# Eight vector additions handed to accumulating GpSimd transfers, with a new instruction order: attention fused with a gated FFT convolution on one Trainium2 core

## The chip, the cores and the metric

The kernel runs on one core of one Trainium2 chip. The time is the device time of one execution in microseconds (us). The engines are TensorE (PE), VectorE (DVE), ScalarE (ACT), GpSimd (POOL) and SyncE (SP); each works through its own instructions in the order in which they were emitted, and waits on semaphores for the others. DMAs are issued by SP and ACT (hardware queues) and by GpSimd (a software queue), and run on the core's 16 DMA engines.

## The reference, cut to what matters

```python
# attention: batch 4, 8 heads, 768 positions, 64 per head
scores = scale * q @ k^T + bias(head, distance)      # bias falls with the distance
keep   = (pos < 8) | (0 <= row - pos < 96)           # 8 global keys and a window of 96
a      = softmax(where(keep, scores, -1e9))
x      = (a @ v), heads joined                       # [4, 768, 512]
# gated convolution over the sequence
x1, x2, x3 = split(x @ w_proj, 3)                    # 512 columns each
X2 = rfft(x2, n=768, axis=1);  H = rfft(filter_fft, n=768, axis=0)
y  = x1 * irfft(X2 * H, n=768, axis=1) * x3
return (y @ w_out).astype(float32)                   # [4, 768, 512]
```

The part that the change touches is `X2 * H`, a product of complex numbers, and the last folding steps of `irfft`.

## The kernel before

The work of each of the four batches (index `b` from 0 to 3 in the code; the text of the change calls index 1 batch 2 and index 2 batch 3) is an attention part and a convolution part. The program puts the attention of batch `b + 1` among the convolution of batch `b`.

**Attention.** The 768 positions are cut into key tiles of 112, in three groups (`GRP`). GpSimd loads q, k and v from HBM, casting float32 to float16 (`load`, L325). PE turns q and k tiles (`turned`, L679; the very first tiles come in float32 and are turned at L647), then computes scores for a pair of heads (`scores`: the biases of the first batch at L707, the scores at L720), with 64 rows per matmul, two heads side by side. ACT takes the exponentials (L748), DVE multiplies by a mask (L760), PE multiplies by v (`values`, L778 and L783), DVE takes reciprocals and scales (`xn`, L802, L808), PE turns the result (`trx`, L825) or SP does by a transposing DMA (`crossed_x`). `gate` (L870) projects x1 and x3; the gates `g` are their product (L881).

**Convolution.** DVE folds the turned x (`butterfly`, L846 to L857). The projection of x2 (L944) is evacuated to `ab`. `spectra` makes spectra on PE (`forward`, L634) with short Fourier matrices: six slots `X[:, 0..5]` of 512 columns. Slots (0, 1) and (2, 3) are real and imaginary parts of a complex product with the filter: DVE multiplies X by the filter's real part `h1` into `p1`, by `h2` (imaginary part, once with a minus sign) into `p2`, and adds `p1` and `p2` with its two halves swapped into X (`sums`, L1098). Slots 4 and 5 are done apart (L1081, L1084). PE then goes back (`inv`, L965 and L968; three slots and `p3` per matrix) into `eo`. `mixed` unfolds `eo` on DVE: `u` and `w` (sums and differences of the odd parts, L1036 and L1037), `t = z - u` (`mt`, L1038), `u` doubled (`mu`), `z = z + u` (`mz`, L1040), `s = t - w` (`m1`, L1041), `t = t + w` (`m2`, L1042). `gated` joins even and odd parts (`half`, L1056 and L1057) and multiplies with the gates (L1061). `out` projects with `w_out` (L996), the result is evacuated to `ot` and stored by SP (L1003). The in-place `z` and `t` are parts of `eo` of 128 columns at a step of 384; X, `p1` and `p2` are contiguous over two slots, 1024 float16 numbers per partition.

**The order.** Every step is an operation (`Op`) of a plan, numbered in the order in which `graph` creates it, with the engines that may do it, a cost for the planner, what it reads and writes. `ORDER` is a string that was written by a search outside the program. Each of its words is an operation number, the engine that does it (P, A, V, G, S) and, for matmuls, the PSUM banks. `schedule` reads it and the operations are emitted one after the other, so the words of one letter are that engine's program:

```python
n = next(i for i, x in enumerate(word) if x in "PAVGS")
o, at = self.ops[int(word[:n])], [int(x) for x in word[n + 1:]]
o.eng = word[n]
assert o.eng in o.cost
```

A word such as `i13b0` puts 13 matmuls on idle data at the start. Semaphore waits are put in by the framework from the data that instructions read and write. The numbers that matter here: 523 and 536 are the sums of batch index 1, 752 and 765 those of index 2; 563 and 565 are `mz` and `m2` of index 1, 792 and 794 those of index 2; 543 to 557 and 772 to 786 are the `inv` matmuls behind the sums, 566 and 795 the first `half` behind `mz` and `m2`; 45 is the load of q tile 5 of the first batch and 154 its turning on PE; 43, 44 and 49 to 51 are loads of v tiles 2 to 6 of the first batch, 258 to 262 the first loads of the second batch, 718 to 739 loads of the last one.

Of the kernel before, what the change touches and what calls it, by code (L numbers as in the profile page):

```python
# [13 lines left out]
Alu = mybir.AluOpType  # L14
Act = mybir.ActivationFunctionType

P = 128
# [14 lines left out]
def dve(n, rate=1, psum=False):  # L32
    return 0.068 + (0.005 if psum else 0.0) + n / rate / 960.0
# [4 lines left out]


ORDER = """  # L40
4V 0S 1A 2S 3A 21G 12V 13V 28V 10G 30A 29A 31A 15V 33V 11A i13b0 76P0 32A 34G 17G 19V 41G 18G 9V 40G 39G 42G 20V 66A
63A 24V 61A 72P1 46G 14V 35G 25V 70P2 26V 23A 22V 7G 64A 47G 73A 48G 45G 67A 60A 38G 77V 86P45 80V 74P3 52G 44G 90P01
43G 16V 75V 71A 78P2 79V 50G 49G 110P6 111V 51G 91P 81A 65A 62A 112P3 113A 88P 87P 89A 55G 261G 108P2 8V 219P6 220A
92P 93A 114P3 156P7 94P45 96P 109V 95P 27V 115V 122P23 262G 97A 69V 260G 221V 157V 214P0 82P45 259G 222V 123A 158P7
159V 84P 116P23 215A 216V 160P1 117A 83P 161V 120P67 53G 217V 154P1 5V 155V 118P23 258G 270G 85A 269G 121A 119A 268G
36S 267G 162P01 273G 98P67 275G 68V 99V 100V 37S 164P45 163A 165A 103P23 104V 105V 276G 166P67 167A 168P01 274G 124P23
125V 126V 129P45 130V 131V 56G 57G 169A 106P6 107A 101P7 102A 127P2 128V 175P01 176V 132P3 58G 133V 170P45 59G 139P3
145P2 263G 223A 54G 177V 178P0 171V 362P1 493G 492G 172V 173P4 224A 179V 227V 229P5 207V 226A 266G 277G 141A 174V
360P0 491G 272G 218A 134P3 208V 201V 271G 363A 230A 361A 364A 150P4 185P0 228V 186P1 358P7 489G 490G 147A 6A 278G 210V
200V 203V 188A 209V 231V 359V 202V 211V 225V 152A 181P2 136A 232A 140P1 369P67 142V 375P45 204V 183A 279G 143V 370A  # L50
390P3 135P2 388P1 499G 498G 212V 365A 501G 376A 500G 187V 137A 391V 389V 372P67 180P0 366P23 373A 392P45 191P1 138V
182A 374V 264S 434P0 436P6 367A 371V 393A 193A 395P23 189V 396A 510G 438P7 435V 205V 398P45 399A 196P0 437V 439V
449P67 450A 401P23 402A 198A 184V 507G 504G 206V 285P1 281P4 394V 213V 506G 286A 505G 283P5 446P23 440P01 397V 443P67
282A 447A 296P4 307P2 284A 298P3 297A 289P4 441A 299A 149P5 144P0 302P3 592P1 290A 400V 494G 151A 195P5 300P4 451V
509G 444A 265S 377V 368V 722G 146A 403V 234V 235V 236V 237V 383P67 448V 308A 190P0 502G 303A 238V 153V 301A 239V 148V
192A 384V 240V 197A 378P23 721G 385V 287P4 241P0 593A 590P5 242A 379V 409P67 723G 591A 194V 246P1 247A 380V 288A 442V
404P23 243P0 244A 248P5 726G 588P1 724S 410V 411V 199V 412P4 405V 249A 594V 719G 445V 406V 457P67 381P5 245V 595A 250V
407P0 589A 408A 382A 452P23 386P1 387A 458V 233V 459V 618P0 460P5 619A 453V 738G 413V 454V 251P67 252A 461V 496S 620P1
621V 508G 255P23 305V 253A 420P0 257A 455P1 292V 456V 256A 631P67 632A 605P45 294P3 422A 295A 414P1 416A 495S 664P0
254V 665A 304V 666P2 482V 668P3 667A 602P67 603A 735G 483V 669V 424P1 484V 306V 309P0 310A 478P2 425P3 528P0 280G 485V  # L60
291V 606A 679P45 486V 480A 426A 311V 427A 529A 676P67 419P2 677A 415P3 293V 417A 421A 511P0 607V 512A 312V 680A 487V
524P1 525A 313P0 462P2 418V 670P67 678V 428V 604V 681V 728G 599P45 464A 321P3 733G 323P1 314A 322A 600A 671A 515P2
315P3 516A 325P0 324V 317P1 318A 327P4 488V 326V 429P5 328A 497G 430P0 319P2 320A 431A 432A 601V 736G 513P1 514A 316V
628P23 633V 596P45 673P67 672V 597A 629A 730G 526P0 674A 329V 463P1 468P4 465A 330V 473P5 475A 625P23 626A 622P67 846S
734G 890S 821P1 848S 729G 527A 423V 331V 433V 732G 334V 727G 332V 472P5 623A 539P2 630V 477P3 519P0 845S 335V 333V
822V 847S 540A 467P1 520A 720G 474A 819P2 737G 338V 336V 470V 339V 469A 517P0 337V 479A 627V 537P5 518A 613P67 614V
820A 538A 349P1 350A 718G 598V 615V 889S 624V 675V 817P0 532P2 818A 340P5 503G 685P67 686V 824V 341A 533A 687A 608P01
609V 530P5 531A 823V 892S 610V 471V 891S 682P23 683V 476V 639P01 640V 684V 346P4 347A 634P67 616P5 617A 641V 828P23
829A 855P01 856A 635V 611P4 535V 343P5 893P23 688S 894A 636V 612V 481V 902P67 344A 852P01 355P4 903A 830V 853A 534V
637P2 541V 638V 642P3 643V 352P5 542V 649P3 689S 904V 356A 353A 834P67 835A 521V 825P01 826A 522V 854V 654P2 656A  # L70
655P5 739G 645P4 647A 644P6 690S 523V 657A 651A 466V 536V 659P2 661A 712V 711V 646A 648V 702P7 704A 714V 858P45 859A
896P23 713V 831P01 832A 697P6 857V 715V 345S 897A 543P7 707P4 709A 836V 557P5 555P0 556A 744P1 551P2 545P4 553P3 699A
716V 860V 348S 549P0 650P6 558A 550V 833V 554A 717V 827V 658V 725S 544A 552A 731G 547P5 342S 548A 546A 560V 559V 753P0
691P7 895V 849P45 652A 754A 850A 899P23 693A 900A 755P6 756A 660P0 745A 561V 837P45 838V 839A 740P7 851V 840P23 757P6
564V 701P1 841V 842V 662A 901V 843S 351S 703A 861P23 908P45 898V 905P01 741A 565V 862V 692P7 758A 909V 910A 863V 696P6
357S 906V 562V 864P23 907V 706P0 759P1 694A 563V 761P7 865V 866A 568V 742P4 743A 762A 766P5 768P2 569V 767A 844S 566V
911S 585P3 663V 354S 746P4 567V 760A 764V 867S 579P7 912S 748P1 769A 582P2 573P5 708A 763V 580A 868S 770V 749A 570P7
747A 583A 576P2 765V 705V 771V 750V 774P4 786P1 586A 782P3 571A 751V 913S 775A 778P7 870P0 710V 752V 577A 783A 787A
935V 934V 936V 772P2 780P4 773A 781A 937V 930P3 932A 776P2 777A 938V 872A 784P1 785A 885P4 880P3 958P0 779A 789V 945P7
939A 788V 940V 941P1 959A 946A 790V 791A 943P0 944A 653V 875P7 695V 942A 954P2 578S 955A 949P0 950A 793V 877A 956P1  # L80
957A 947P2 948A 572S 794V 792V 967P7 968A 587S 869P0 581S 969P1 970A 882A 795V 797V 924P2 796V 951V 971V 960P7 961A
952V 962P1 963A 925P3 871A 927A 879P7 881A 915P0 972V 953V 884P3 584S 965V 988P7 887A 964V 698A 574A 886A 966V 888V
973P6 974A 700V 992P4 993A 989A 873V 798V 805P1 994P6 995A 990P3 975P4 991A 997V 996V 977P5 978A 979P7 980A 874P6
802P3 808P7 883V 876A 799P6 998V 814P5 878V 976A 981V 982V 575S 999A 926A 914P2 806A 1001V 811P1 983V 984A 1002V 1000V
929P4 917A 815A 800A 801S 919P6 807S 986V 803A 809A 920P7 985V 987V 1005V 816S 810S 1003V 804S 1006V 812A 931A 1004V
1013P3 1018V 916A 813S 921A 933V 918V 922A 1007P2 1008A 1016V 1009S 923V 1014A 1015S 928V 1017V 1010P7 1019V 1020P2
1011V 1012S 1021V 1022S 1023P3 1024A 1026P7 1027A 1025S 1028S 1029P2 1030A 1031S
"""


# [109 lines left out]
class Fused:  # L200
# [725 lines left out]
    def conv(self, b):  # L926
        nc, g, DM, S = self.nc, self.g, self.DM, self.S
        h, last = S // 2, b == self.B - 1
        g.batch = (self.PERIOD * b, self.PERIOD)
        X, y, w = self.X, self.y, self.w  # L930
        q3 = math.sqrt(0.75)
        for i in range(2):
            if (b, i) in self.PAIR_AB:
                self.projected(i)
            for t, (src, key, k) in enumerate((
# [6 lines left out]
                def proj(_, src=src, bk=bk):  # L942
# [7 lines left out]
                    name="ab")  # L950
# [4 lines left out]
        for jp in range(2):  # L955
            eo, ke = self.eo[:, 2 * jp:2 * jp + 2], ("eo", jp)
# [17 lines left out]
                        after=self.early if b == 0 else ())  # L974
            if last or jp:
                js = (jp,) if last else (0, 1)
                self.mixed(js)
                for half in range(0 if last else 2):
                    self.gated(b, js, half)
        osc = 1.0 / (S * H_SCALE * X1_SCALE)  # L980
        for t in range(6):
# [6 lines left out]
            o = self.outs % 6  # L988
            self.outs += 1
            past = tuple(g.readers.get(("ot", o), ()))  # L990
            for c0, cw in ((0, DM // 2), (DM // 2, DM // 2)) if last and t == 5 else ((0, DM),):
                bk = g.bank()

                def project(_, t=t, bk=bk, cs=slice(c0, c0 + cw), cw=cw):
                    for c in range(4):
# [3 lines left out]
                     name="out")  # L999
# [65 lines left out]
    def spectra(self, b, pair):  # L1065
        nc, g, X, DM = self.nc, self.g, self.X, self.DM
        n = pair[0] // 2
# [12 lines left out]
        if n == 2:  # L1080
# [11 lines left out]
        g.op("V", dve(1024, 2), lambda _: nc.vector.tensor_mul(  # L1092
            p1, xs, self.h1[:, pair[0]:pair[0] + 1].to_broadcast([P, 2, DM])),
             r=rs, w=[("p1", k)], name="prod")
        g.op("V", dve(1024, 2), lambda _: nc.vector.tensor_mul(p2, xs, self.h2[:, o:o + 2]),
             r=rs, w=[("p2", k)], name="prod")

        g.op("V", dve(1024, 2), lambda _: nc.vector.tensor_add(xs, p1, p2[:, ::-1]), r=[("p1", k), ("p2", k)],  # L1098
             w=[("X", s) for s in pair], name="sums")


    def run(self):
        e = mybir.EngineType
# [132 lines left out]
```

## Time and profile before

| what | value |
|---|---|
| runs | 164.96, 167.73, 165.4 us; median 165.4 |
| profiled execution | 165.6 us, its span 163.9 us, clock 1.0 |
| PE busy | 156.0 us (95%), 1619 matmuls |
| DVE busy | 149.6 us (91%), 339 instructions |
| ACT busy | 149.7 us (91%), 325 instructions |
| POOL busy | 73.9 us (45%), 101 instructions |
| GpSimd's DMA queue | 74960 packets, 11.82 MB |

The span goes from the first to the last instruction of the program in one profiled execution; the execution's own time is a little longer. Busy time is the union of an engine's instructions. An instruction on DVE or ACT overlaps the next by a few hundredths, so the distance between starts is what one costs in a row of such. PE's ends are modelled: the distance of starts tells its rate. The profile names DMA issues on GpSimd as instructions of POOL; the last of them starts at 80.26 us.

### The profile page before, as it was taken

Reading aid. Unit: us, or ns where it says so; the run is one execution under the profiler, and the core shown is the slowest. Engines: PE = TensorE matmul, PEld = TensorE weight load, DVE = VectorE, ACT = ScalarE, POOL = GpSimd, SP = SyncE. Lnnn points to the kernel's source line nnn. Section 1 sums busy time; section 2 is a strip of 40 time slices with the busy share of each in tenths; the row PEclk is TensorE's granted clock in tenths of the full one; section 3 lists DMA queues with packets and bytes.
Section 4 is the critical chain, followed back from the end, with each engine's and each line's share of the span. In section 5 each row is a group of like instructions: output and inputs, shape, how many; then the busy total and the mean of one; then the engine's idle time right before and its main releaser. Section 6 shows DMA issues by size and latency. Waiting matters only on the chain.

```text
span 163.9 us, 4281 instructions
## 1 busy us (share of the span) xinstructions
PE 156.0 (95%) x1619; PEld 95.3 (58%) x1619; DVE 149.6 (91%) x339; ACT 149.7 (91%) x325; POOL 73.9 (45%) x101
## 2 busy tenths in 40 slices
PE   6798999999999999899999999999999999999990
PEld 2455678665456875455566755665754654574550
DVE  3788869999999999999999999999999999999970
ACT  4688899999999999999999999999999798999931
POOL 7999999985599999978700000000000000000000
PEclk9999999999999999999999999999999999999999
DMA  4999999999999999999995545000444270010586
GB/s 109 196 147 125 166 172 166 158 173 206 178 173 158 153 150 146 140 172 155 156 139 102 76 93 184 14 0 4 130 128 107 78 270 0 4 64 0 206 326 238
DMA packets 91684, 21.97 MB, mean 134 GB/s; under 512 B 84288, under 2 KB 88720, under 8 KB 91664
## 3 DMA queue, kind: packets, MB, share of 16 engines
q0 software_dynamic: 74960, 11.82, 98.7%
q1 hardware_dynamic: 14624, 9.37, 21.0%
q10 hardware_dynamic: 2080, 0.52, 1.8%
q8 instruction: 12, 0.20, 0.4%
q14 instruction: 8, 0.07, 0.1%
HBM read 24.64 MB, written 6.29 MB: 189 GB/s over the span
## 4 chain that ended last, share of the span: by engine, by line
PE 55%; DVE 25%; POOL 6%; ACT 5%; DMA 4%; issue 2%; POOLq 0%; ACTq 0%; DVEq 0%
PE bank L870 16%; PE bank L996 12%; PE bank L944 8%; DVE E L760 5%; PE bank L634 4%; DMA qn<-in_q_dram 4%; DVE xn L802 3%; PE bank L720 3%; PE bank L778 3%; PE bank L965 3%; POOL kn L325 3%; PE bank L783 2%; PE bank L707 2%; ACT E L748 1%; DVE xT L309 1%
## 5 line engine op out<-in xcount | busy, mean ns | idle before, releaser
L870 PE MATMUL bank<-xT,w 128*128 128x384 f16 x256 | 48.5, 326 | 0.6 <-DVE KT L309 0.6
L748 ACT ACTIVATE E<-bank 128x832 f16<-128x832 f32 (+2 forms) x64 | 44.6, 785 | 1.2 <-PE bank L720 1.2
L870 PEld LDWEIGHTS <-w 128*128 128x128 f16 x256 | 23.6, 98 | 17.1 <-issue 1.9
L325 POOL DMA_DIRECT2D vn<-in_v_dram x28 | 23.4, 852 | 4.0 <-DMA wo<-in_moe_w_out_dram 1.7
L325 POOL DMA_DIRECT2D kn<-in_k_dram x27 | 22.7, 866 | 0.7 <-issue 0.3
L996 PE MATMUL bank<-wo,y 128*128 128x512 f16 (+1 forms) x100 | 22.9, 370 | 0.0
L760 DVE TENSOR_TENSOR E<-E,mask 128x832 f16<-128x832 f16 (+1 forms) x36 | 21.4, 617 | 0.4 <-ACT E L748 0.4
L325 POOL DMA_DIRECT2D qn<-in_q_dram x21 | 19.0, 920 | 1.4 <-PE bank L944 1.4
L879 ACT CAST g<-bank 128x384 f16<-128x384 f32 x30 | 15.8, 542 | 0.3 <-PE bank L870 0.3
L313 ACT ACTIVATE x<-bank 128x384 f16<-128x384 f32 x31 | 16.1, 548 | 0.0
L313 ACT ACTIVATE ot<-bank 128x512 f32<-128x512 f32 (+1 forms) x23 | 12.9, 608 | 3.1 <-PE bank L996 1.9
L802 DVE TENSOR_TENSOR xn<-bank,rc 128x512 f16<-128x512 f32 (+1 forms) x20 | 15.2, 763 | 0.2
L778 PE MATMUL bank<-vn,E 128*128 128x65 f16 x224 | 15.3, 193 | 0.0
L313 ACT ACTIVATE ab<-bank 128x512 f16<-128x512 f32 x24 | 15.1, 688 | 0.1
L996 PEld LDWEIGHTS <-y 128*128 128x128 f16 x100 | 9.4, 98 | 9.9 <-issue 0.3
L778 PEld LDWEIGHTS <-E 128*128 128x128 f16 x224 | 14.0, 97 | 1.9
L783 PE MATMUL bank<-vn,E 128*128 128x65 f16 x192 | 15.0, 193 | 0.0
L720 PE MATMUL bank<-QT,KT 64*128 64x208 f16 (+1 forms) x224 | 14.9, 245 | 0.0
L309 ACT CAST X<-bank 128x512 f16<-128x512 f32 x24 | 14.0, 659 | 0.1
L783 PEld LDWEIGHTS <-E 128*128 128x128 f16 x192 | 13.2, 97 | 0.8 <-issue 0.2
L309 ACT CAST eo<-bank 128x384 f16<-128x384 f32 x28 | 12.4, 566 | 0.8 <-PE bank L968 0.8
L720 PEld LDWEIGHTS <-KT 64*128 64x128 f16 x224 | 8.4, 94 | 6.4 <-issue 3.9
(158 smaller groups left out, 337.4 us busy)
## 6 DMA issues: line engine op xcount, KB each, us to landing
out_dram<-ot SPq DMA_DIRECT2D x23, 256.0 KB, 2.5
qn<-in_q_dram POOLq DMA_DIRECT2D x21, 128.0 KB, 5.7
vn<-in_v_dram POOLq DMA_DIRECT2D x24, 112.0 KB, 5.7
kn<-in_k_dram POOLq DMA_DIRECT2D x23, 112.0 KB, 5.6
w<-in_moe_w_proj_dram POOLq DMA_DIRECT2D x4, 256.0 KB, 6.4
ot<-in_q_dram ACTq DMA_DIRECT2D x2, 256.0 KB
w<-in_moe_w_proj_dram POOLq DMA_DIRECT2D x1, 512.0 KB, 7.8
wo<-in_moe_w_out_dram POOLq DMA_DIRECT2D x1, 512.0 KB, 8.1
```

Of the source, the lines that this page charges most:

```text
L309: {"A": nc.scalar.copy, "V": nc.vector.tensor_copy, "G": nc.gpsimd.tensor_copy}[e](out, in_)
L313: self.nc.scalar.mul(out, in_, c)
L325: return self.g.op(eng, 0.57 + 0.00035 * nbytes[0] if eng == "G" else 0.5, lambda _: e.dma_start(dst, src), w=w, r=r, nbytes=nbytes, name= ...
L720: nc.tensor.matmul(bs[hh].f32()[:, off:off + w], self.KT[hs, hp, P * m:P * m + P], self.QT[hs, hp, KL * m:KL * m + w], start=(off == 0 and ...
L748: nc.scalar.activation(dst, src(), Act.Exp, scale=self.scale)
L760: g.op("V", dve(w, 2), lambda _: nc.vector.tensor_mul(eo, eo, mk), r=[("mask", 2 * hp), ("mask", 2 * hp + 1)], w=[("E", hp, gi)], name="ma ...
L778: nc.tensor.matmul(o[:, n, hh], ef[:, at:at + P], vt[:, t, 2 * hp + hh, 0:D + 1], start=first, stop=(t == 0), skip_group_check=True)
L783: nc.tensor.matmul(o[:, n, hh], ef[:, at:at + P], vt[:, t - 1, 2 * hp + hh, 0:D + 1], start=False, stop=True, skip_group_check=True)
L802: nc.vector.tensor_mul(to, o[:, :, :, 0:D].rearrange("p i (t h) d -> p i t h d", h=2), rc.rearrange("p i (t h) o -> p i t h o", h=2).to_br ...
L870: nc.tensor.matmul(bk.f32()[:, 0:h], self.w[:, c, o + P * j:o + P * j + P], self.xT[:, c, h * s:h * s + h], start=(c == 0), stop=(c == 3))
L879: first = g.op("AV", {"A": act(h), "V": 0.0005}, lambda e: nc.scalar.copy(x3, pts[1].f32()[:, 0:h]) if e == "A" else None, use=[pts[1]], w ...
L996: nc.tensor.matmul(bk.f32()[:, 0:cw], y[:, c, P * t:P * t + P], self.wo[:, c, cs], start=(c == 0), stop=(c == 3))
```

## The change

For batch indices 1 and 2 (`ACC`), eight additions of 128 x 1024 float16 numbers leave DVE and become DMAs of GpSimd that add their source to what stands in the destination, both in SBUF. `accumulate` makes them. For the sums of products, the product with `h2` goes first and is written with its halves swapped, the product with `h1` is written over X, and the transfer adds `p2` to X. For `mz` and `m2` the transfer adds `u` to `z` and `w` to `t`. The cost of 1.1 and the service time `svc` are the planner's bookkeeping for the search. The whole order is new: operations of all engines stand in another sequence, and some evacuations and copies change between ACT and DVE.

```diff
+    ACC = (1, 2)
+
+    def accumulate(self, out, in_, r, w, nbytes, name):
+        o = self.g.op("G", 1.1, lambda _: self.nc.gpsimd.dma_start(out, in_, accum_op=Alu.add),
+                  r=r, w=w, nbytes=nbytes, name=name)
+        o.svc = 0.0007 * nbytes[1]
+
-    def mixed(self, js):
+    def mixed(self, b, js):
...
+        eos = [("eo", jp, jj, par) for jp in js for jj in range(2) for par in range(2)]
...
-        op(lambda _: v.tensor_add(z, z, u), ("mt", "mu"), "mz")
+        if b in self.ACC:
+            self.accumulate(z, u, [(k, jp) for k in ("mt", "mu") for jp in js] + eos,
+                            [("mz", jp) for jp in js], (128, 512 * n * 2), "mz")
+        else:
+            op(lambda _: v.tensor_add(z, z, u), ("mt", "mu"), "mz")
         op(lambda _: v.tensor_sub(s, t, w), ("hi", "lo", "mt"), "m1")
-        op(lambda _: v.tensor_add(t, t, w), ("hi", "lo", "mt", "m1"), "m2")
+        if b in self.ACC:
+            self.accumulate(t, w, [(k, jp) for k in ("hi", "lo", "mt", "m1") for jp in js] + eos,
+                            [("m2", jp) for jp in js], (128, 512 * n * 2), "m2")
+        else:
+            op(lambda _: v.tensor_add(t, t, w), ("hi", "lo", "mt", "m1"), "m2")
...
+        h1 = self.h1[:, o:o + 1].to_broadcast([P, 2, DM])
+        if b in self.ACC:
+            g.op("V", dve(1024, 2), lambda _: nc.vector.tensor_mul(p2[:, ::-1], xs, self.h2[:, o:o + 2]),
+                 r=rs, w=[("p2", k)], name="prod")
+            g.op("V", dve(1024, 2), lambda _: nc.vector.tensor_mul(xs, xs, h1),
+                 w=[("X", s) for s in pair], name="prod")
+            self.accumulate(xs, p2, [("p2", k)], [("X", s) for s in pair], (128, 2048), "sums")
+            return
```

Of the order, the words that the text speaks of. GpSimd's program at the start, before and after:

```diff
-21G 10G 34G 17G 41G 18G 40G 39G 42G 46G 35G 7G 47G 48G 45G 38G 52G 44G 43G 50G 49G 51G 55G 261G 262G 260G 259G
+17G 18G 34G 42G 7G 40G 10G 39G 21G 41G 48G 35G 47G 46G 45G 38G 43G 44G 53G 261G 258G 262G 259G 260G 49G 50G 51G 52G
```

Here 7, 10, 17, 18 and 21 are the index row, the identity, the row number, the distances `dg` and the mask `far`; the others are loads. At the end of GpSimd's program, where the old string ends with `503G 739G 731G`, the new one has:

```diff
+508G 720G 733G 731G 536G 738G 523G 563G 565G 752G 765G 792G 794G
```

In the new string the words of PE between a product and the first inverse matmul behind its sum are, for 523: `654P5 644P0 645P1 553P5 855P23 858P67 549P0 655P1 660P5 707P0 545P4 896P23 849P67 557P5 744P0`, then `543P6`. The words of scores (82 to 96, 116 to 122 and their like in later batches) form 30 runs on PE in the old string and 33 in the new one, of which 21 and 26 stand behind the turning of q tile 5 (154). On idle data there are 12 matmuls instead of 13.

More of the change, by code (lines that the diff above doesn't have):

```diff
@@ new lines @@
+373A 175P23 176V 365A 177V 228A 170P45 171V 375P01 233V 376A 266G 172V 377V 134P7 178P2 139P3 136A 138V 272G 173P7
+142A 271G 179V 366P45 141A 143V 174A 200V 491G 367A 388P6 201V 208V 207V 389A 203V 209V 210V 390P2 391A 180P7 374V
+181P3 183A 185P4 187A 186P6 211V 489G 368V 401P23 188A 402A 182A 144P5 202V 146A 212V 398P01 399A 278G 150P6 204V 205V
+438P7 439A 403V 189V 392P23 400V 393A 436P5 395P01 437V 394V 224V 434P4 206V 435A 279G 504G 145P7 147A 396A 226V 149P2
+443P45 506G 148V 190P7 505G 152A 507G 501G 264S 151A 192A 213V 446P01 447A 184V 196P6 198A 449P23 191P7 193A 444A
@@ new lines @@
+440P01 494G 234V 235V 441A 236V 237V 448V 195P6 294P7 295A 281P4 298P5 309P7 285P0 153V 592P1 282A 450A 238V 310A 499G
+239V 240V 248P7 445V 296P4 397V 286A 500G 442V 593A 594V 383P01 194V 384V 197A 249A 378P23 283P6 297A 299A 385V 386P4
+379V 380V 199V 284A 307P7 308A 265S 498G 404P01 387A 590P6 250V 381P5 409P23 405V 382A 591A 726G 588P4 589A 406V 407P5
+410V 451V 452P01 251P67 408A 253A 411V 457P23 412P5 252A 595V 453V 454V 413A 287P7 288A 496S 458V 459V 246P4 247A
+455P6 243P5 244A 722G 255P23 257A 664P4 665A 254V 721G 456V 245V 460P7 302P5 461V 303A 666P3 668P7 311V 667A 241P4
@@ new lines @@
+242A 736G 256A 482V 723G 424P5 300P6 301A 618P3 619A 620P4 730G 669V 483V 484V 485V 304V 426A 420P2 422V 289P6 486V
+290A 291V 419P7 421A 305V 621A 724S 718G 528P5 529A 515P3 516A 625P67 626A 679P01 430P5 432A 312V 511P3 306V 680A
+323P5 292V 293V 324A 319P4 732G 487V 320A 512A 425P6 502G 313P7 321P5 423V 427V 488V 322A 317P2 318V 428V 315P4 316A
+325P0 326V 314A 681V 414P3 416A 327P2 328A 719G 330V 596P45 622P67 623A 329V 597A 280G 628P01 624V 331V 526P3 527A
+513P2 514A 510G 627V 629A 429P4 467P3 431A 334V 332V 469A 415P2 335V 676P01 417A 602P45 333V 603A 631P67 632A 677A
@@ new lines @@
+826A 471V 636V 891S 893P01 894A 642P6 688S 689S 355P7 356A 643V 537P4 827V 637P6 352P5 902P01 834P23 466V 538A 638V
+353A 903A 831P67 521V 541V 481V 649P4 522V 835A 654P5 536G 542V 904V 644P0 645P1 725S 656A 690S 646V 553P5 647V 648V
+832A 833V 855P23 858P67 554A 712V 856A 549P0 550A 711V 714V 655P1 738G 713V 715V 651A 859A 836V 660P5 662A 657V 716V
+707P0 545P4 896P23 849P67 709A 850A 851V 557P5 744P0 523G 546A 897A 543P6 857V 717V 745A 757P7 658V 544A 348S 551P4
+758A 547P2 650P3 558A 552A 860V 555P6 556A 898V 740P0 548A 559V 755P5 652A 742P4 560V 741A 756A 743A 357S 828P23 829A
@@ new lines @@
+852P01 853A 899P67 895V 561V 701P5 562V 563G 830V 345S 900A 753P4 754A 564V 840P23 841V 842V 748P0 761P1 854V 762A
+565G 703A 697P6 699A 746P4 901V 837P23 838V 759P5 653V 839V 659P1 861P67 843S 749A 747A 750V 760A 908P23 862V 342S
+661A 751V 752G 763V 702P1 704V 905P45 863A 909V 910A 764V 691P0 906V 907V 693A 692P6 566V 706P7 696P4 864P23 766P0
+765G 768P5 694A 567V 570P6 767A 865V 866V 769A 349P0 571A 576P6 663V 770V 771V 780P5 776P2 844S 350A 708A 774P7 698A
+568V 777A 911S 867S 569V 784P0 785A 912S 786P4 573P3 868S 700V 772P0 787A 773V 775A 778P4 913S 781A 782P2 783V 779A
@@ new lines @@
+585P7 788V 789V 790V 793V 586A 574A 579P2 791A 792G 935V 874P7 879P3 876A 577A 934V 937V 884P0 578S 870P4 575S 880P7
+882A 875P6 877A 915P5 945P7 946A 936V 872A 958P6 938V 939V 940V 959V 941P7 943P4 6A 794G 944A 942V 351S 705V 881A
+956P6 957A 878V 947P4 695V 948A 949P3 954P1 950A 967P4 955A 883V 710V 572S 795V 354S 962P3 963A 960P6 961A 587S 952V
+869P1 968A 969P3 970A 951V 953V 965V 964V 925P7 927A 971V 886A 582P4 580A 871A 966V 972V 885P3 797V 887A 583A 919P0
+917A 581S 921A 929P1 796V 973P3 975P4 976A 979P5 980A 977P2 978A 990P0 798V 992P7 994P4 988P6 974A 982V 991A 993A 981V
@@ L88 @@
+989A 995A 873V 920P5 983V 984A 802P3 888V 997V 996V 914P7 916A 799P4 800A 986V 930P0 998V 999A 987V 805P2 1001V 931A
+808P4 985V 801S 932A 1000V 811P0 1002V 933V 1005V 803A 1003V 814P3 1006V 584S 924P1 806A 807S 1004V 922A 809A 810S
+812A 804S 815A 816S 923V 1007P0 1010P3 926A 1018V 1016V 1013P1 928V 918V 1019V 813S 1017V 1008V 1011A 1012S 1009S
+1014A 1015S 1023P3 1024A 1025S 1020P2 1021A 1026P3 1027V 1022S 1028S 1029P1 1030A 1031S
 """
@@ L1091, in spectra @@
         rs = [("X", s) for s in pair] + [("h", s) for s in pair] + [("h", o + 1, 0)]
[L1092 to L1094 removed]
+        h1 = self.h1[:, o:o + 1].to_broadcast([P, 2, DM])
[6 more added lines that the diff above has]
+            return
+        g.op("V", dve(1024, 2), lambda _: nc.vector.tensor_mul(p1, xs, h1), r=rs, w=[("p1", k)], name="prod")
         g.op("V", dve(1024, 2), lambda _: nc.vector.tensor_mul(p2, xs, self.h2[:, o:o + 2]),
```

62 lines of the change are left out of this document (14 added, 48 removed).

## The prediction

> **What bounds the kernel now.** I read the shares of the page first, then the engines by stage, then the spacing of matmuls in the timeline, then the chain of waits, last the DMA issues.
>
> ```profile
> span 163.9 us, 4281 instructions
> PE 156.0 (95%) x1619; PEld 95.3 (58%) x1619; DVE 149.6 (91%) x339; ACT 149.7 (91%) x325; POOL 73.9 (45%) x101
> q0 software_dynamic: 74960, 11.82, 98.7%
> ```
>
> Three engines are above 90%, so the shares can't say which one sets the time; the third line shows that GpSimd's own queue, which carries the loads, takes as much as all 16 DMA engines for the span. By stage:
>
> ```profile
> core 0: us, PE busy (x) PEld busy (x) DVE busy (x) ACT busy (x) POOL busy (x), PEclk, DMA share, GB/s
> 40.00:75.00 35.00, 34.16 (x381) 21.28 (x380) 34.73 (x74) 34.65 (x69) 31.03 (x38) 1.00 2.14 160
> 75.00:100.00 25.00, 24.98 (x288) 15.49 (x288) 24.63 (x54) 24.65 (x56) 6.12 (x8) 1.00 1.27 123
> 100.00:130.00 30.00, 30.00 (x300) 18.36 (x299) 29.86 (x58) 29.09 (x79) 0.00 (x0) 1.00 0.27 71
> ```
>
> From 100 us on PE has no idle time, at full clock, and GpSimd is free. A busy PE need not be a fast one, so look at the spacing:
>
> ```profile
> 98.25 0.81 PE L870 MATMUL bank<-xT,w 128*128 128x384 f16 x4
> 98.99 0.53 PE L720 MATMUL bank<-QT,KT 64*128 64x208 f16 x8
> 99.46 4.07 PE L870 MATMUL bank<-xT,w 128*128 128x384 f16 x24
> ...
> 103.46 0.75 PE L720 MATMUL bank<-QT,KT 64*128 64x208 f16 x14
> ```
>
> The 24 gate matmuls run from 99.46 to 103.46, less a gap of 0.10 at the end: 0.1625 us each for 384 columns, 0.42 ns per column. Score matmuls (64 rows) run in pairs side by side, 0.087 us a pair. Four matmuls from 98.25 end at 98.90, the scores start at 98.99; their four pairs end at 99.34, the gates start at 99.46. So a run of scores among other work costs PE 0.09 + 0.12 = 0.2 us on top. Counting all matmuls at these rates gives 144.0 us of work; PE streams nearly all the time, and only its lost time can be won.
>
> ```profile
> 10.51 1.54 POOL kn L325 x2
> 12.05 5.91 DMA qn<-in_q_dram
> 17.97 0.05 issue
> 18.01 0.40 PE bank L679 x4
> ```
>
> The chain shows the last point where a load holds PE: the first batch's q tile 5, issued by GpSimd at 12.05, landed after 5.91 us, turned on PE at 18.01. In the old order 133.4 us of PE work begins there, and PE ends at 159.9. So 159.9 - 18.0 - 133.4 = 8.5 us are lost behind it: 21 runs of scores at 0.2 are 4.2 us, the other 4.3 us are waits, few of them long.
>
> **The change.** Eight DVE adds go: two sums of products and two in-place sums (`mz`, `m2`), in batches 2 and 3 (indices 1 and 2).
>
> ```profile
> 99.88 0.68 DVE L1095 TENSOR_TENSOR pp<-X,h 128x1024 f16<-128x1024 f16 x1
> 100.48 0.58 DVE L760 TENSOR_TENSOR E<-E,mask 128x832 f16<-128x832 f16 x1
> 100.98 0.68 DVE L1098 TENSOR_TENSOR X<-pp 128x1024 f16<-128x1024 f16 x1
> ```
>
> *Removed.* Such an instruction shows 0.68, but the next starts 0.60 later: 8 x 0.60 = 4.8 us of DVE. All eight lie after 98 us, in the stage where PE has no gap. The direct worth on the path is 0.
>
> *Products.* There are still two per pair of slots; the second now writes X in place, same shape, so 0.
>
> *Engines swapped by the new order.* I compared each operation's letter in the two strings. ACT loses 4.2 us, DVE gains 2.4 (by the rows of the same work, less the overlap with the next: on DVE 0.55 for a cast of 384 columns, 0.37 for a copy of 448, 0.69 and 0.94 for `xn`). DVE is 2.4 us lighter in all, ACT 4.2. What can this win? The waits of PE that a DVE result ended, KT at 66.1 (0.61) and eo at 75.0 (0.23), 0.8 together. Bounds: 0 (they lie ahead of all removed adds) and 2.0 (half of the 4.3). I take -0.8.
>
> *PE order.* After q tile 5 the new string leaves 134.0 us of PE work instead of 133.4 (the same matmuls, fewer ahead of it): +0.5. It splits the scores into 26 runs from there on instead of 21: 5 x 0.2 = +1.0. One warm-up matmul less lies ahead of the first loads: 0.
>
> *POOL's queue.* The same nine loads and the same mask and identity work stand ahead of q tile 5, in another order. By their rows (0.77 to 0.97 a load, 1.24 for `far`, 0.51 the identity, 1.13 `dg`, 0.72 `irow`) it is issued at 12.25 instead of 12.05: +0.2. First-batch v tiles 4 to 6 now stand behind five loads of the next batch: v6 is issued at 22.4 instead of 18.2, lands at 27.9 (5.5 us, the row of such loads), and PE comes to need it 9.3 us of work and six runs behind q tile 5, at 28.7. Hidden by 0.8 us; without that cover it is one for one.
>
> *The eight transfers.* They stand at the end of POOL's queue, whose loads were all issued by 81 us, so each is issued when its inputs are ready; only the load of v tile 5 of the last batch stands between the first two. Behind them on POOL nothing else waits. What waits is, for sums, PE's inverse matmul (L965), in order, with everything behind it; for `mz` and `m2`, DVE's `half` (L1056), and the masks, evacuations and products queued behind it on DVE. PE work in the new string between the start of the last DVE operation ahead and the first consumer: 8.0, 6.8, 7.4 and 6.5 us for the four sums; 8.4, 7.5, 10.8 and 11.6 for the others. Less that operation (0.60, or 0.36 for the doubling), a sum has at least 5.9 us from issue to landing. The profile has no accumulating transfer, so bounds from rows:
>
> ```profile
> out_dram<-ot SPq DMA_DIRECT2D x23, 256.0 KB, 2.5
> qn<-in_q_dram POOLq DMA_DIRECT2D x21, 128.0 KB, 5.7
> w<-in_moe_w_proj_dram POOLq DMA_DIRECT2D x4, 256.0 KB, 6.4
> wo<-in_moe_w_out_dram POOLq DMA_DIRECT2D x1, 512.0 KB, 8.1
> ```
>
> The sums move 256 KB in rows of 2 KB, as the stores do: 2.5 us is the low bound. High is 8.1: 512 KB (an accumulation reads twice) through POOL's queue while it is full. After 85 us that queue is empty, so the sums are nearer the stores, plus POOL's 0.9 us to issue and the second read: I take 4.5, under 5.9, and charge 0, covered by the gates, values and out projections that the new order puts there. The in-place sums have rows of 256 B, 1024 of them, as the q loads; I take 5.7, under 6.9 or more: 0.
>
> The Trainium skill (DMA: Bandwidth & Descriptors, Anatomy of one DMA) gives about 2.0 us plus bytes over 436 GB/s for a GpSimd transfer, an estimate of 2.6 us here; by it the charge would be 0 with more room. The rows of this case (5.7 for 128 KB in a full queue) don't follow it.
>
> The skill also has a rule against the change (SBUF — State Buffer, Who interferes with whom): GpSimd can't write descriptors while DVE holds their shared port in its fast copy modes. The trace doesn't bear it out: the timeline has two k loads in 1.65 us at 7.3 us, with DVE 60% busy, and four in 3.35 at 69.4, with DVE full, 0.83 and 0.84 each; by the rule they would differ, by the rows the sum would not change.
>
> **Sum**, against the profiled execution's 165.6 us (span 163.9 and 1.7 around it; the median is 165.4): -0.8 + 0.5 + 1.0 + 0.2 + 0 = +0.9, so 166.5 us. With the bounds of the waits alone: 165.3 to 167.3.
>
> **Rivals.**
>
> *Late transfers (slower).* An accumulation takes longer than the 5.9 us that the order leaves it. At 8.1 us the sums keep PE waiting for 0.6 + 8.1 - 6.8 = 1.9 us in batch 2 and 0.6 + 8.1 - 6.5 = 2.2 in batch 3, and `m2` of batch 2 keeps DVE for 1.2. PE has no slack to take that back, so 166.5 + 4.1 = 170.6, up to 172. For it: read and write of the destination, short rows, the transposes of SP at 115 to 127 us on the same engines. Against it: an empty queue. It decides from 5.9 us on and is a slowdown by over 2% from some 7.
>
> *Late loads at the head (slower).* The moved v tiles 4 to 6 and weight pieces land 2 to 3 us later than by the median, since the queue is full there. PE then stands at 28.7 us: some 169.
>
> *The waits go (faster).* With DVE and ACT lighter, the 4.3 us of waits fall by 2 us more, and the added runs of scores overlap other waits: 166.5 - 2.5 = 164.0. A gain over 2% (3.3 us, about what a measurement of this kernel can tell from no change) is nearly excluded: q tile 5 at 18.2, 134.0 of work, 26 runs at 0.2, the last store's 4.0 and 1.7 outside give 163.1 with no other wait at all. Only an earlier q tile would break that floor.
>
> *The relief isn't used.* The adds go, but the chain after 100 us is PE's, and the order stays as good as the old one: 165.6. This lies inside my forecast's range.
>
> **Chances.** Forecast with the unused relief 0.49, its own range 164.8 to 168.3; late transfers 0.32; late loads 0.08; waits gone 0.11. Of the late transfers about a sixth ends under 168.7, of the late loads a third; of the last case a third passes 2%. Faster by over 2%: 0.04. Slower: 0.27 + 0.05 + 0.06 from the forecast's upper end = 0.38. Within 2%: 0.58. The range reaches half way into each side case: 163.6 to 171.0.
>
> **What would show it.** Right: PE busy 30.0 of 30 in 100 to 130, DVE's busy time lower by 2 to 3 us, ACT's by about 4, the turn of q tile 5 near 18.2, transfers that land under 5.9 us after issue, no PE wait on a DMA behind L965. Wrong: PE waiting for a transfer ahead of L965, or DVE ahead of L1056, by a microsecond or more (late transfers); a PE gap near 28 us on a vn load (late loads); a q tile 5 turned before 17 us, which would void the floor.

## Result: 11% slower, and the profile after

The changed kernel takes 183.4 us (median of four executions, 181.66 to 183.78) against 165.2 us: ratio 1.109, interval 1.100 to 1.118. The forecast of 166.5 us was wrong, and so was its range. The profiled execution took 181.66 us. The ratios leave out executions that took over 1.5% longer than the fastest of their kernel, and where such an execution was the profiled one (plain copies, sums as transfers with in-place sums on DVE, identity first), landings, packets and the order of events alone are read from its trace.

The page of the changed kernel:

```profile
span 180.0 us, 4265 instructions
PE 160.5 (89%) x1618; PEld 97.2 (54%) x1618; DVE 149.6 (83%) x336; ACT 147.6 (82%) x309; POOL 83.4 (46%) x109
PEclk9999999999999999999969999999999999969999
q0 software_dynamic: 79696, 13.92, 103.5%
```

PE, DVE and ACT are all busy for a smaller share of the span than before, so nobody became the bound: something makes them wait. The clock row has two dips to 6, at slices 21 and 36 (of 4.5 us each). By stage:

```profile
core 0: us, PE busy (x) PEld busy (x) DVE busy (x) ACT busy (x) POOL busy (x), PEclk, DMA share, GB/s
75.00:100.00 25.00, 21.64 (x244) 13.46 (x244) 19.96 (x43) 20.45 (x48) 8.96 (x11) 0.93 1.65 119
100.00:130.00 30.00, 28.19 (x303) 17.27 (x299) 27.54 (x54) 28.76 (x69) 6.09 (x6) 1.00 0.72 100
130.00:180.00 50.00, 40.17 (x242) 22.22 (x242) 35.50 (x75) 29.92 (x64) 3.15 (x2) 0.96 0.59 133
```

PE lacks 3.4 us in the first stage, ahead of all eight transfers, 1.8 in the second and most in the last. The waits, in us in total, times, and longest, name what ended them:

```profile
DVE y L1072 <- DMA eo<-mix: 7.0, 2, 4.9
...
PE bank L778 <- DMA vn<-vn: 3.6, 2, 3.4
...
PE bank L965 <- DVE X L1100: 2.7, 1, 2.7
...
PE bank L996 <- DVE y L1077: 1.9, 1, 1.9
...
PE bank L965 <- DVE X L1119: 1.6, 1, 1.6
PE bank L965 <- DMA X<-pp: 1.4, 1, 1.4
```

Two causes stand here. `vn<-vn` is no transfer of the change: it is SP's copy of the global keys' values (495), which `values` (L778) needs. And DVE stood twice at `half` (L1072 here) for an in-place sum, `eo<-mix`; three of PE's waits at L965 and L996 are for DVE results that come after it. The last line is PE waiting for a sum of products itself (`X<-pp`): the second one of batch index 2, which stands behind the in-place sums in GpSimd's queue. The chain that ended last (start, us) has both transfers as its longest pieces behind one of 15 us without a shown wait:

```profile
83.29 6.41 DMA vn<-vn
...
142.15 10.91 DMA eo<-mix
```

The second one is `m2` of batch index 2 (794). DVE's timeline around it, with the idle time before an instruction in brackets:

```profile
148.00 0.63 DVE L881 TENSOR_TENSOR g<-g,x 128x384 f16<-128x384 f16 x2 [0.18 <-ACT x L313]
153.50 0.69 DVE L1072 TENSOR_TENSOR y<-eo 128x1024 f16<-128x1024 f16 x1 [4.88 <-DMA eo<-mix]
...
154.44 0.69 DVE L1117 TENSOR_TENSOR pp<-X,h 128x1024 f16<-128x1024 f16 x1
```

DVE was at `half` at 148.6, 6.5 us after the transfer's issue; the transfer took 10.9. The last line is what makes it dear: the products of the last batch (L1117) are queued behind `half`, and PE's inverse waits for their sums. PE waited 1.73 us at 154.6 and 2.89 at 156.6.

GpSimd issued the pair of index 2 late, when ACT had doubled `u` for `mz` (`mix`, 1.06 us from 139.90):

```profile
141.25 3.15 POOL L1024 DMA_DIRECT2D eo<-mix  x2 [15.11 <-ACT mix L313]
```

The last DVE operation ahead of `m2` had also started at 139.90, but `m2` went out behind `mz`, at 142.15, 2.25 us later.

The landings, issue to landing by the trace: sums of batch index 1 3.8 and 4.3 us, then `mz` 5.4 and `m2` 8.1; sums of index 2 6.9 and 9.3, `mz` 7.8 and `m2` 10.9. The DMA traffic from 141.0 to 153.2 (packets, MB, share of 16 engines; and per issue KB and median us to landing) says why:

```profile
q0 software_dynamic: 2080, 0.52, 55.3%
q1 hardware_dynamic: 864, 1.57, 39.4%
...
out_dram<-ot SPq DMA_DIRECT2D x6, 256.0 KB, 5.2
eo<-mix POOLq DMA_DIRECT2D x2, 256.0 KB, 9.3
```

GpSimd's two transfers are some 2050 packets of 256 bytes, a packet per row. They hold 55.3% of 16 engines for 12.2 us: 108 us over 2080 packets, 52 ns each. SP's stores at the same time (864 packets of 1.8 KB on average) show 89 ns each. So 256 bytes of an accumulation cost more than half of what a store pays for 1.8 KB, each in-place sum fills the queue for 1024 x 0.052 / 16 = 3.3 us by itself, and the two queues together hold 95% of the engines.

### The profile page after: what moved, and what is told of

It reads as the page before. It is cut to its first block, busy times and chain, and to the rows that moved or that the text cites. A ratio compares the mean times of both kernels' runs of the same rounds, so it can differ in the third digit from the quotient of the medians.

```text
span 180.0 us, 4265 instructions
## 1 busy us (share of the span) xinstructions
PE 160.5 (89%) x1618; PEld 97.2 (54%) x1618; DVE 149.6 (83%) x336; ACT 147.6 (82%) x309; POOL 83.4 (46%) x109
## 3 DMA queue, kind: packets, MB, share of 16 engines
q10 hardware_dynamic: 2080, 0.52, 1.6%
## 4 chain that ended last, share of the span: by engine, by line
PE 36%; DVE 19%; DMA 14%; issue 12%; ACT 10%; POOL 5%; SPq 1%; POOLq 0%; ACTq 0%; DVEq 0%
PE bank L870 11%; DMA vn<-vn 6%; DMA eo<-mix 6%; PE bank L944 6%; PE bank L996 3%; PE bank L720 3%; DVE E L760 3%; PE bank L634 3%; ACT E L748 3%; PE bank L679 2%; PE bank L965 2%; ACT ot L313 2%; PE bank L778 2%; DVE xn L802 2%; DMA out_dram<-ot 2%
## 5 line engine op out<-in xcount | busy, mean ns | idle before, releaser
L748 ACT ACTIVATE E<-bank 128x832 f16<-128x832 f32 (+2 forms) x64 | 45.1, 773 | 1.0 <-PE bank L720 0.7
L996 PE MATMUL bank<-wo,y 128*128 128x512 f16 (+1 forms) x100 | 23.1, 370 | 2.2 <-DVE y L1077 1.9
L760 DVE TENSOR_TENSOR E<-E,mask 128x832 f16<-128x832 f16 (+1 forms) x36 | 21.5, 619 | 0.1
L1024 POOL DMA_DIRECT2D eo<-mix x4 | 6.3, 1906 | 28.2 <-ACT mix L313 15.1
L778 PE MATMUL bank<-vn,E 128*128 128x65 f16 x224 | 15.4, 194 | 3.6 <-DMA vn<-vn 3.6
L313 ACT ACTIVATE ot<-bank 128x512 f32<-128x512 f32 (+1 forms) x23 | 13.4, 611 | 6.2 <-PE bank L996 4.5
L778 PEld LDWEIGHTS <-E 128*128 128x128 f16 x224 | 14.1, 98 | 6.0 <-issue 4.6
L802 DVE TENSOR_TENSOR xn<-bank,rc 128x512 f16<-128x512 f32 (+1 forms) x21 | 15.8, 759 | 0.6 <-DVE rc L808 0.2
L996 PEld LDWEIGHTS <-y 128*128 128x128 f16 x100 | 9.4, 98 | 11.8 <-DVE y L1077 2.7
L313 ACT ACTIVATE ab<-bank 128x512 f16<-128x512 f32 x22 | 13.3, 653 | 2.7 <-PE bank L944 2.7
L879 ACT CAST g<-bank 128x384 f16<-128x384 f32 x26 | 13.8, 538 | 0.6 <-PE bank L870 0.6
```

The lines of the kernel that those rows point to most:

```text
L313: self.nc.scalar.mul(out, in_, c)
L748: nc.scalar.activation(dst, src(), Act.Exp, scale=self.scale)
L760: g.op("V", dve(w, 2), lambda _: nc.vector.tensor_mul(eo, eo, mk), r=[("mask", 2 * hp), ("mask", 2 * hp + 1)], w=[("E", hp, gi)], name="ma ...
L778: nc.tensor.matmul(o[:, n, hh], ef[:, at:at + P], vt[:, t, 2 * hp + hh, 0:D + 1], start=first, stop=(t == 0), skip_group_check=True)
L802: nc.vector.tensor_mul(to, o[:, :, :, 0:D].rearrange("p i (t h) d -> p i t h d", h=2), rc.rearrange("p i (t h) o -> p i t h o", h=2).to_br ...
L879: first = g.op("AV", {"A": act(h), "V": 0.0005}, lambda e: nc.scalar.copy(x3, pts[1].f32()[:, 0:h]) if e == "A" else None, use=[pts[1]], w ...
```

## Experiments

Line numbers shift by up to three in most of the kernels below: `half` is then L1069, `values` L775. Differences in us are of medians; by the ratios, each against the kernel before measured beside it, they come out up to 0.6 us smaller or larger. "Idle of PE" is the spacing of matmuls' starts beyond the rate of their shape.

**New order, eight additions left out.** How much of the loss is the order alone?

```diff
-        o = self.g.op("G", 1.1, lambda _: self.nc.gpsimd.dma_start(out, in_, accum_op=Alu.add),
+        o = self.g.op("G", 1.1, lambda _: None,
```

> The new order with the eight additions left out altogether: no transfer and no DVE addition in their places (so X, z and t lack one term in batches 2 and 3). Theory 1, two causes: the order alone costs 4.8 us (3.5 of PE waiting at 86 us for the copy of the global v rows, and 1.3 of matmuls at half rate behind it) and some 0.9 for its runs of scores, the rest is the transfers': 165.2 + 5.7 = 171. Theory 2, the order is all of it: 180 or more. Theory 3, the transfers are all of it: 164.5 to 165.5.

Measured 170.6 us, ratio 1.030 (1.023 to 1.036). The wait for the copy is still there:

```profile
PE bank L778 <- DMA vn<-vn: 4.1, 2, 3.2
```

So about 5 us of the 18 are the order's, and it costs them without any transfer of the change.

**Old order, the same additions left out.** Is the relief of DVE worth anything?

```diff
+        op(lambda _: None if b in (1, 2) else v.tensor_add(z, z, u), ("mt", "mu"), "mz")
...
+        lambda _: None if b in (1, 2) else nc.vector.tensor_add(xs, p1, p2[:, ::-1])
```

> The old order with the same eight additions left out and nothing in their places (the same terms are lacking). It gives what the relief of DVE could be worth at most. Theory 1 (PE has no gap where they stand): 164.7 to 165.2 us, within 0.3% of before. Rival (DVE sets the pace there): up to 8 x 0.60 = 4.8 us less, 160.4.

Measured 165.1 us, ratio 0.998 (0.996 to 1.001): under half a per cent. By stage (columns as above), DVE is 2.6 us lighter in 100 to 130, and PE, full before, stays full:

```profile
100.00:130.00 30.00, 30.00 (x303) 18.54 (x302) 27.27 (x53) 29.13 (x79) 0.00 (x0) 1.00 0.27 73
```

**New order, the additions on DVE.** `ACC = ()`, and the eight words become DVE words, each right behind its last input.

> The new order with the additions as DVE instructions, each right behind its last input on DVE, and no transfers. Theory 1: as without the additions, or up to 1.5 us more: 171 to 172.5. Theory 2 (order): 180. Theory 3 (transfers): 166.

Four executions took 174.2, 177.8, 178.8 and 179.4 us; no ratio can be given. Even the fastest is above what was expected. Beside the wait for the copy (3.0 us), its trace has PE waits of 1.1 us each at 118.5, 125.8 and 140.5, all for DVE: the new order has no room on DVE for this work. Why the others are slower was not settled.

**The copy moved back.** One word of the new order: 495 stands right behind 496, as in the old order, ahead of the turns of the last batch. SP's timeline after the change shows what it stood behind:

```profile
80.62 2.62 SPq L669 DMA_TRANSPOSE KT<-kn  x2
83.29 0.71 SPq L325 DMA_DIRECT2D vn<-vn  x1
```

The two transposing transfers had to wait for k loads of the last batch, which landed up to 80.5 us; in the old order the copy went out with 496, at 67.4 us.

```diff
-503G 848S 480A ... 671A 495S 468P5
+496S 495S
```

> The changed kernel with one word moved: the second copy of global v rows of batch 3 (495) stands on SP right behind the first (496), as in the old order, ahead of the two transposing DMAs that it stood behind. Theory 1: PE's wait at 86 us and the half rate behind it go, 183.4 - 4.8 = 178.6. Rival: the later waits on the transfers take the time up, since DVE and POOL have their own lateness there: 182 to 183.4.

Measured 177.8 us, ratio 1.073 (1.066 to 1.079): 5.6 us back for one word, where 4.8 had been expected. It is the base of the experiments that follow. The long wait at `half` is as it was:

```profile
DVE y L1069 <- DMA eo<-mix: 7.0, 2, 5.1
```

**On this base, the additions left out.**

> The new order with the copy of the global v rows moved ahead (as in new_vglobal) and the eight additions left out, with nothing in their places (X, z and t lack one term in batches 2 and 3). Theory 1: the two costs add up, so the new order without its late copy and without transfers is as good as the old one, 170.6 - 4.8 = 165.8 us. Rival: with the early wait gone another one takes its place: 168 or more.

Measured 168.1 us, ratio 1.017 (1.013 to 1.021). So the eight transfers cost 9.7 us, and the order, its copy mended, still 2.8, where 0.6 had been expected: a miss, and the rival's figure of 168 came. Without the transfers the copy was worth 2.1 us by the ratios (1.030 against 1.017), with them 5.6. Part of the difference is the matmuls at half rate behind the wait in the changed kernel (1.3 us, last section). Another part is what the rival said: with the wait of 3.3 us gone, PE waits 1.4 us at 95 us, for an evacuation by ACT and a transposed k tile. The rest is not explained.

**On this base, plain copies instead of accumulations** (the same bytes and rows, no addition).

```diff
-  self.nc.gpsimd.dma_start(out, in_, accum_op=Alu.add)
+  self.nc.gpsimd.dma_start(out, in_)
```

> As new_vglobal, but each of the eight transfers is a plain copy of the same shape instead of an addition (it overwrites X, z or t). Theory 1 (an accumulating packet takes twice the time of a plain one: 178 ns against 86 for 2 KB; 53 against some 25 for 256 B): the in-place transfers land 2 to 4 us sooner and the sums don't queue behind them so long; 177.8 becomes 169 to 172. Rival (the time is issue and completion, whatever the packets do): 176 to 178.

Measured 168.1 us, ratio 1.014 (1.009 to 1.020), below the 169 to 172 expected and no more than with nothing there. Sums landed after 2.7 to 3.2 us, in-place sums after 3.3 to 5.5; the trace has packets of 4096 bytes, many rows in one. Accumulations went out row by row. The cost is not the bytes, the queue or the wait for inputs; it is accumulating in this form.

**On this base, long rows.** `eo` and `mix` laid out so that `z`, `t`, `u` and `w` are contiguous, 2 KB per partition: 128 rows per transfer instead of 1024. Everything is computed; on DVE two operations per unfolding become four.

```diff
-        self.eo = t("eo", [P, 4, 2, S // 2])
+        self.eo = t("eo", [P, 3, 4, 2, P])
-        self.mix = t("mix", [P, 4, 2, 2, P])
+        self.mix = t("mix", [P, 2, 4, 2, P])
...
-        z, t, s = (eo[:, :, :, P * m:P * m + P] for m in (0, 2, 1))
+        z, t, s = (eo[:, m] for m in (0, 2, 1))
```

> As new_vglobal, but eo and mix are laid out so that z, t, u and w are 2 KB contiguous per partition; the transfers add 128 rows of 2 KB instead of 1024 of 256 B. Four DVE instructions of mixed are split in two each (0.07 us more apiece). Theory 1 (the short rows cost 3.4 us of the queue each, so the pair lands 8 to 11 us after issue and holds up the sums behind it): transfers land 4 to 5 us after issue, DVE's wait ahead of half falls from 7.0 us to under 1, and the time to 168. Rival (accumulation itself or POOL's lateness is what is slow): 175 or more.

Measured 167.5 us, ratio 1.014 (1.010 to 1.019): 10.3 us back for a layout. The DMA traffic of 134 to 148 us, in this kernel:

```profile
q0 software_dynamic: 288, 0.52, 21.5%
q1 hardware_dynamic: 1008, 1.84, 36.3%
...
eo<-mix POOLq DMA_DIRECT2D x2, 256.0 KB, 5.2
```

The same 0.52 MB are 288 packets and 48 us of engine time (21.5% x 16 x 14) instead of 108, beside even more stores; `mz` and `m2` landed 4.4 and 6.0 us after issue, and no wait at `half` is left.

**On this base, sums as transfers, in-place sums on DVE.**

> As new_vglobal, but only the sums of products are transfers; the in-place sums are DVE instructions, each right behind its last input on DVE. Theory 1 (the sums by themselves land in 3.8 to 4.3 us, inside the 5.9 that the order leaves): no PE wait on a transfer; the time is that without additions plus up to 2.4 us of DVE: 166 to 169. Rival (sums are late by themselves): PE still waits 1.6 us ahead of the inverse matmul in batch 3, 171 or more.

Measured 1.028 (1.023 to 1.033), 169.2 to 170.3 us in the executions of the ratio: just above the expected upper end. Landings 3.3 to 5.5 us, and no PE wait for a sum; where PE stood longest, at 95 us, it waited for k tiles that SP transposed.

**On this base, sums as transfers, in-place sums left out.**

> The new order with the copy of vglobal early; the four sums of products are made by transfers, the four in-place sums (mz, m2 of batch indices 1 and 2) are left out. Theory: with nothing ahead of them in GpSimd's queue the sums land in about 4 us, PE never waits for them, and the time equals that with all eight additions left out, 168.1: 167.5 to 168.7. The sums then cost nothing by themselves, and the 170.1 of the kernel with the in-place sums on DVE holds 2 us of DVE work. Rival: the sums as transfers cost by themselves (waits or contention): 170 or more.

Measured 168.3 us, ratio 1.018 (1.014 to 1.023), equal to the kernel without any addition. PE is full from 100 on (columns as above):

```profile
100.00:130.00 30.00, 30.00 (x315) 18.95 (x314) 28.98 (x55) 29.14 (x73) 2.56 (x3) 1.00 0.44 87
130.00:160.00 30.00, 30.00 (x180) 15.85 (x178) 29.46 (x65) 23.30 (x52) 0.00 (x0) 1.00 0.35 127
```

The sums cost nothing: they landed after 4.0, 4.6, 3.7 and 5.7 us. The kernel before this one is slower by the DVE work of four in-place sums (some 1.6 us by the ratios).

**On this base, in-place sums as transfers, sums left out.**

> The new order with the copy of vglobal early; the four in-place sums are made by transfers of short rows as in the change, the four sums of products are left out. Theory: the in-place transfers hold DVE ahead of half by themselves, about 2 us in batch index 1 and 4 to 5 in batch index 2, and what is queued behind it on DVE holds PE: 168.1 + 6 to 8 = 174 to 176. Rival: most of the damage is that the sums of batch index 2 queue behind the in-place transfers of batch index 1; without sums the time is 169 to 171.

Measured 179.0 us, ratio 1.083 (1.078 to 1.088). Expected were 174 to 176: the theory's cause, but 3 us more of it, and no less than the 177.8 with all eight. The rival, that sums queued behind the in-place transfers do most of the damage, is refuted. `m2` of index 2 landed 12.7 us after its issue with no sum in the queue; seven stores of SP ran beside it. DVE's waits for the in-place sums in this kernel:

```profile
DVE y L1069 <- DMA eo<-mix: 8.5, 2, 6.3
```

DVE was at `half` at 143.3 us, 6.5 us behind the issue of `m2` as with all eight transfers, and stood there for 6.3 us. The stage around it (columns as above) has PE at 9.4 of 15 us and the clock at 0.77:

```profile
145.00:160.00 15.00, 9.42 (x65) 6.32 (x63) 10.36 (x20) 8.62 (x21) 0.00 (x0) 0.77 0.20 50
```

**On this base, one DVE word moved.** `half` of index 2 (795) goes behind the last batch's products and sums; the transfers stay as in the change.

```diff
-... 572S 795V 354S ... 952V ... 966V 972V 885P3
+... 572S 354S ... 952V ... 966V 972V 795V 885P3
```

> The new order with the copy of vglobal (495) at its early place and one more edit: in batch index 2 the operation half (795), at which DVE stood 5.1 us for the transfer of m2 (794), moves on DVE behind the sums and products of the last batch (952, 951, 953, 965, 964, 971, 966, 972). Theory: the late transfer is dear through what is queued behind the waiting DVE instruction. DVE's wait there falls to 1 us or less, PE's waits of 1.9 and 2.9 us at 150 to 153 us and the half-rate matmuls behind them go: 177.8 - 4.8 = 173.0, 172 to 174. Rival: PE needs the gated result as urgently as the products of the last batch, so its out projections wait in their place: 176 to 178.

Measured 171.6 us, ratio 1.039 (1.033 to 1.045): 6.2 us back by the medians and 5.6 by the ratios, at the upper end of the 4 to 6 expected. The transfer landed as late as ever, 11.6 us after issue, at 148.79, but DVE was busy until 149.43:

```profile
148.83 0.68 DVE L1097 TENSOR_TENSOR X<-X,h 128x1024 f16<-128x1024 f16 x1
149.43 0.68 DVE L1069 TENSOR_TENSOR y<-eo 128x1024 f16<-128x1024 f16 x1
```

PE's idle times left behind 120 us are 1.97 (`m2` of index 1), 1.46 (a sum that landed after 9.2 us) and 0.84. So in this kernel most of the price of a late transfer is what is queued behind the instruction that waits.

**Long rows, identity first.** An attempt at the rest of the order's cost: the identity matrix (10) moves to the head of GpSimd's program.

> The kernel with the eight additions as transfers of long rows and the early copy of vglobal (167.5), with the identity matrix (10) made first on GpSimd instead of behind five other operations. Theory: part of the 2.5 us that the order still costs is the late identity at the head; the first turns on PE come back from about 7.6 to 7.2 us or earlier and the time falls by 0.4 to 0.8: 166.7 to 167.1. Rival: the head is paced by the loads, which the identity now delays by 0.5 us: 167.5 to 168.

Measured 168.7 us, ratio 1.018 (1.011 to 1.025); 167.1, 168.3 and 169.2 us in the executions of the ratio: no gain. The first turns on PE wait for a float32 copy of the identity. The timeline of the kernel before has it early on ACT:

```profile
4.43 0.28 ACT L309 CAST p<-ident 128x128 f32<-128x128 f16 x1
```

In the timeline of this kernel it is DVE's, behind 24 other instructions:

```profile
7.52 0.35 DVE L306 CAST p<-ident 128x128 f32<-128x128 f16 x1
```

DVE came to it at 7.32 us with the identity late and at 7.52 with it early, because GpSimd made `dg`, for which DVE waits first, 0.4 us later. The releaser that I had named was not the one that came last.

## Why the prediction was wrong, point by point

- **PE is the bound and the relief of DVE is worth 0: shown right**, 0.998 in the old order. The changed kernel had no gain to set against its costs.
- **Moved transfers of SP: omitted.** The working went through the new queues of PE and GpSimd and counted loads, but not SP's, where a copy went behind two transposing transfers. It is a wait that could have been read from the two strings: 495 stands behind 847 and 848 in the new one and ahead of them in the old, and the trace before had the copy at 67 us and the turns at 82. It cost 5.6 us in the changed kernel.
- **Eight transfers at 0: the failing term, by the transfers' size and by what covers them.** For the sums 4.5 us were taken, and 3.8 and 4.3 measured in index 1; without the in-place sums they cost next to nothing (1.018 against 1.017). For `mz` and `m2` 5.7 us were taken from the q loads, which have rows of the same length: measured 5.4 to 10.9. Two things were missing: accumulating rows go one to a packet at some 52 ns, and two such transfers follow one another in one queue, so that the second lands behind 2 x 3.3 us of work, before stores share the engines. The high bound of 8.1 us, by a row of 512 KB, was below what came. The estimate by the Trainium skill (DMA: Bandwidth & Descriptors, Anatomy of one DMA), 2.6 us, lies below every accumulation measured here; 3.3 us was the least.
- **The cover of `m2`: right in index 1, wrong in index 2.** DVE reached `half` 6.0 us behind the issue of `m2` in index 1, near the 7.5 - 0.60 = 6.9 of the working. In index 2 it was 6.5 us, against 11.6 - 0.60 = 11.0. First, `m2` was issued 2.25 us behind the start of the last DVE operation ahead of it, not 0.60: `mz` stood before it and waited for ACT. Second, DVE was at `half` 8.7 us behind that start, where 11.6 us of PE's work had been counted; but `half` is DVE's, and DVE did not wait for all of it. An allowance of 11.0 us would have covered even this landing of 10.9.
- **Its price: mis-sized too.** The rival of late transfers had the mechanism and the place (DVE ahead of `half`, with the products behind), but gave the sums 4.1 us and `m2` 1.2 in index 1 alone, up to 172 us together. The runs show the reverse: sums by themselves nothing, in-place sums 10.9 (1.083 against 1.017), of which some 6 hang on one word behind which the last batch's products wait. The 1.6 us that PE stood for a sum in the changed kernel are also theirs: that sum landed 9.3 us after its issue behind them, and 5.7 without them.
- **The order at +0.9: measured +2.8** with the copy mended. The -0.8 for removed waits is not confirmed: PE's idle time in the slice of 60 to 70 us is 0.8 us less in the kernel without additions, but the wait at 66 us is also gone in the old order without additions, where nothing had changed so early (PE busy 9.89 of these 10 us, against 9.39 before). So its going need not be the change's doing. The q tile 5 was turned at 17.41 us, not 18.2, since it landed after 4.3 us instead of 5.9. But PE loses some 2.5 us more in the first 50 us. That holds some added runs of scores, the late float32 identity (first turn at 7.7 us instead of 7.16) and, in the kernel without additions, 0.9 us of waiting at 20 us for another copy of SP; the prediction saw the first alone, and the parts were not separated.
- **GpSimd's issuing beside DVE: a misread row.** DVE was busy 1.58 of the 1.65 us at 7.3 us, not 60%, so the two rows that were compared both have a full DVE. The load at 3.56 us has it busy 0.30 of 0.84 us, and took the same 0.84; accumulations of 128 rows were issued in 0.88 and 0.90 us beside a full DVE. The 0 taken for it stands, for this kernel.
- **Late loads at the head: no.** No PE gap of over 0.3 us lies near 28 us.
- **Of the marks:** PE is busy 28.19 of 30 us in 100 to 130 (30.0 expected), ACT 2.1 us less (4), DVE 149.6 as before (2 to 3 less), and PE waited for a sum at L965 by 1.6 us (no such wait). In the old order without additions DVE falls to 145.1; in the new one more came to DVE from ACT than was counted (six products with a PSUM operand instead of two, 2.2 us, and two evacuations of `ab`, 1.4, among others).

The 18.2 us are then 5.6 for the copy, 9.7 for the transfers (by the kernels with one kind alone: the in-place ones), and about 3 for the rest of the order, whose cause stays open. No version here beats the kernel before: with the additions free (long rows) the order's cost remains, and with the old order there is nothing to win. The transfers in the old order were not run.

## What to carry to other kernels

Work taken from an engine off the bound is worth nothing, so price the means first: size an accumulating transfer by its packets and by what else its queue and the 16 engines carry at that moment, not by bytes alone; if its rows are short, change the layout before anything else. Count what covers a transfer from its issue, and on the engine that waits for it. For each wait that a change adds or delays, look at what is queued behind the waiting instruction, and move the wait behind what others need. When an order is rewritten, compare every queue, those of the plain copies included, for what now stands behind something that waits.

## What the runs showed of the hardware

- **Accumulating transfers between SBUF and SBUF** cost some 52 ns of an engine per row of 256 bytes and 188 to 198 ns per row of 2 KB (48 and 51 us of engine time for the 256 rows of two transfers), twice the 91 ns of a store's row of 2 KB (81 us for the 896 rows of seven stores, beside the long rows). GpSimd was 1.5 to 2.25 us at issuing 1024 rows, 0.9 at 128. The Trainium skill (DMA: Bandwidth & Descriptors, Why small descriptors are slow) says that transfers within SBUF don't suffer from small descriptors; for accumulations these rows contradict it: 4.9 bytes per ns and engine in short rows, 10 to 11 in long ones.
- **Waits of PE can cost twice.** Behind the wait of 3.52 us at 86 us, six matmuls of 512 columns came 0.43 us apart instead of 0.22, 1.3 us in all, with a granted clock of 0.62 from 90 to 93.5; behind the two of 1.73 and 2.89 us it was 0.58 from 160 to 163. After 3.3 us (additions left out) and after 2.0 us it did not fall. The Trainium skill (TensorE: Matmul & The Clock Gate, Part 1) gives a free-running window of about 3.4 us of idleness after which the clock is halved; the single waits agree with it. The pair of 1.73 and 2.89 us, with two matmuls between, shows that neither wait has to be that long by itself.
